# Layer 2, second block: the products with w_ch1 of a step, then its products with w_ch2 in one stretch

## The chip, the cores and the metric

One core of a Trainium2 chip runs the whole program. The metric is the device time of one execution in microseconds (us), the median of several. TensorE (PE) does the matmuls, VectorE (DVE), ScalarE (ACT) and GpSimd (POOL) the work around them, and SyncE (SP) issues every DMA of the kernel from one queue, in program order.

## The reference, cut to what matters

A retention layer makes `x` of 4 batches of 576 rows and 512 columns; a first gated layer (w_in, w_sg, w_out) follows, and then layer 2, which the change is about:

```python
xn = (x - mean) / sqrt(var + 1e-6) * g_ln            # over the 512 columns
out = x + maximum(xn @ w_ch1, 0) @ w_ch2             # w_ch1: 512 x 2048, w_ch2: 2048 x 512
```

All results are wanted near float32 accuracy. The kernel splits every operand of a matmul into a high half (rounded by the copy) and a low half (operand minus high half), and does three matmuls in place of one: high by high, high by low, low by high.

## The kernel before

The 2304 rows of layer 2 are 18 tiles of 128, in three blocks of six (`TB`). Each block goes through eight steps `p`, so there are 24 steps `s`; a step makes 256 of the 2048 hidden columns for the block.

**The products with w_ch1** are done with seven block products in place of eight (Strassen-Winograd). `hidden(s)` does them: each of the seven is six matmuls of 384 columns into a PSUM bank, 42 matmuls in all, and DVE and ACT put the seven together. The order is w = 0, 5 | 1, 2 | 3, 4 | 6, with a `yield` at each bar. `relu` writes the high half of one of the four hidden tiles (ACT) and its low half (DVE, line 1176).

**The products with w_ch2** of blocks 0 and 1 are `project(s, q)`, q = 0 to 3: nine matmuls of 512 columns each, into six banks that a block holds for all its eight steps (`o_t`). So two of the eight banks are left for the products with w_ch1 in steps 1 to 16. In the main loop each of the four parts of `hidden(s)` is followed by one `project(s - 1, q)`, in steps 1 to 16. Block 2 (steps 16 to 23) is done by `hidden_kept`, which keeps its hidden values, and `multiply_kept` does their products with w_ch2 after step 23.

**What runs beside it.** `split_w2` makes the halves of a 128 x 512 piece of w_ch2 (ACT line 944, POOL line 945), `load_w2` fetches the next piece, `save_w2` writes the halves back to DRAM for block 2, `fetch_w1` brings the split w_ch1 two steps ahead. `turning` prepares combinations of w_ch2 for block 2: load, four subtractions (POOL, line 961), four copies (ACT, line 964), four subtractions (POOL, line 967), store. `ahead(blk, q)` with q from 0 to 31 prepares the next block: rows are loaded and normalized (`norm`: DVE, POOL and ACT), turned (DVE, line 994), stored (`z_dram`), loaded as features, scaled, mixed (`mix_features`, POOL line 1029) and split (`split_features`, ACT line 1036, low half on line 1037 by DVE for block 0 and by POOL for blocks 1 and 2). `load_rest` fetches the rows that the output is added to (DVE, line 1276).

Every engine runs its instructions in the order in which this code emits them; the schedule is written out by hand.

Of the kernel before, what the change touches and what calls it, by code (L numbers as in the profile page):

```python
# [101 lines left out]
def kernel(  # L102
# [36 lines left out]
    def f(ap):  # L139
        return ap.bitcast(F32)  # L140
# [804 lines left out]
            pool.tensor_tensor(out=t[:, 1], in0=raw, in1=f(t[:, 0]), op=ALU.subtract)  # L945

    def save_w2(s):
        if NF <= s < 2 * NK:
            p, i = divmod(s - NF, 2)
# [23 lines left out]
    def row_tile():  # L973

        rows.rotate(-1)
        return rows[-1]

    def load_y(n):
        yh[n] = row_tile()
        nc.sync.dma_start(out=yh[n], in_=y_dram[n])  # L980

    def norm(p, n):
        z = yh[n]

        def stats():
            st = numbers(p)
            yield from rstd(p, st, z, 1e-6)
            after(1, lambda: newton(st))

            def rest():  # L990
                normed(z, st)
                yield
                t = row_tile()
                dve.transpose(out=t, in_=z)
                nc.sync.dma_start(out=z_dram[n], in_=t)

            after(2, rest)

        after(0, stats)
# [23 lines left out]
    def mixed(i):  # L1023
        return mix_at[i % len(mix_at)].rearrange("p (k q c) -> p k q c", k=2, c=32)
# [6 lines left out]

    def split_features(blk):
        b11, b21, b12, b22 = halves(blk)
        for i, y in ((0, b11), (4, mixed(0)), (5, mixed(1)), (6, mixed(2)), (2, mixed(3)), (1, b21), (3, b22)):
# [138 lines left out]
    def relu(s, i, v):  # L1173
        t = h_t[s, i] = h_at[i][s % len(h_at[i])]
        act.activation(out=t[:, 0], in_=v, func=ACTF.Relu)  # L1175
        dve.scalar_tensor_tensor(  # L1176
            out=t[:, 1], in0=v, scalar=0.0, in1=f(t[:, 0]), op0=ALU.max, op1=ALU.subtract
        )

    def hidden(s):  # L1180


        u = t2.tile([128, TH], F32, tag="u", name="u")
        t = t2.tile([128, TH], F32, tag="v", bufs=1, name="t")
        bk = {}
        for part in ((0, 5), (1, 2), (3, 4), (6,)) if s else ((5, 0, 2, 4), (1,), (3,), (6,)):
            for w in part:
                x, a, first, last = HIDDEN[w]
                if first:
                    bk[a] = bank()  # L1190
                product(s, bk[a], w, x, first, last)
                v = bk[a][:, 0:TH]
                if w == (0 if s else 5):
                    act.copy(u, v)
                elif w in (0, 5):
                    dve.tensor_tensor(out=u, in0=v, in1=u, op=ALU.add)
                elif w == 2 or w == 4:
                    dve.tensor_tensor(out=t, in0=v, in1=u if w == 2 else t, op=ALU.add)
                    if w == 4:
                        relu(s, 3, t)  # L1200
                else:
                    if w != 1:
# [3 lines left out]
                    relu(s, {1: 0, 3: 2, 6: 1}[w], v)  # L1206
                if last:
                    free(bk[a])
            yield

    def hidden_kept(s):

# [35 lines left out]
    def turned_row(t):  # L1248
        return t.rearrange("p (k f c) -> p f k c", k=KE, c=32)
# [9 lines left out]
    def project(s, q):  # L1259

        blk, p = divmod(s, NQ)
        i, h = divmod(q, 2)
        t = h_t.pop((s, q))
        if p == 0 and q == 0:
            o_t[blk] = [bank() for j in range(TB)]
        first, last = p == 0 and i == 0, p == NQ - 1 and i == 1
        w = w2_at[i]
        for j in reversed(range(TB // 2)):
# [3 lines left out]
            if last:  # L1272
                n = blk * TB + h * TB // 2 + j

                o = row_tile()
                dve.tensor_tensor(
                    out=turned_row(o), in0=ps.rearrange("p (f k c) -> p f k c", k=KE, c=32),
                    in1=o_s.pop(n).rearrange("p (f k c) -> p f k c", k=KE, c=32), op=ALU.add,
                )
                free(ps)  # L1280
                store_row(n, o)

    def load_rest(n):
        o_s[n] = row_tile()
# [109 lines left out]
    def ahead(blk, q):  # L1394

        tick()
        background(int(PACE[B][q % 4]) if blk == 0 and q > 3 else 0)
        n = (blk + 1) * TB
        if q == 1 and blk:
            for j in reversed(range(TB // 2, TB)):  # L1400
                load_rest((blk - 1) * TB + j)
        if blk + 1 < NB:
            for j in range(TB):
                at = 3 + 5 * j // 2
                if q == at - (j > 0 and blk):
                    load_y(n + j)
                if q == at + 1 + (blk if j == 0 else 0):
                    norm(t2, n + j)
            if q in (13, 20):
                load_features(blk + 1, q // 20)  # L1410
            if q in (15 + blk, 22 + blk):
# [12 lines left out]
            if q >= 24 and q != 28:  # L1424
                if q > 24:
                    next(feat[0], None)
                next(feat[1])
        if q == 4 * NQ - 1:
            for j in reversed(range(TB // 2)) if blk + 1 < NB else range(TB):
                load_rest(blk * TB + j)  # L1430
            if blk + 1 == NB:
                o_s[None] = row_tile()

    def keep():
        t = t4[0].tile([128, 28 * TH], F32, tag="fe", name="kept")
# [27 lines left out]
    for s in range(NB * NQ):  # L1463
        if s == NK:
            keep()
        steps = hidden(s) if s < NK else hidden_kept(s)
        for q in range(4):
            next(steps)
            if 0 < s <= NK:
                project(s - 1, q)  # L1470
            if s >= NQ:
                next(turns, None)

            if q == 0 and s > 1:
                split_w2(2 * s - 1)
            if q == 1 and s > 1:
                load_w2(2 * s + 1)
                save_w2(2 * s - 1)
            if q == 2 and s:
                split_w2(2 * s)  # L1480
            if q == 3 and s:
                load_w2(2 * s + 2)
                save_w2(2 * s)
            if s and q == 2:
                save_w1(s + 1, 0)
# [8 lines left out]
            if s == NB * NQ - 1:  # L1494
# [4 lines left out]
                if q == 3:  # L1499
                    split_kept(4)  # L1500
                    split_kept(5)
            ahead(*divmod(4 * s + q, 4 * NQ))
            if q < 2 and s:
                split_w1(s + 1, q)
            if s < 2 and q > 1 - s and q < 4 - s:
                save_w1(s, q - 2 + s)
            if q == 0:
                fetch_w1(s + 1, 3)
            else:
                fetch_w1(s + 2, q - 1)  # L1510
    for _ in multiply_kept(NB - 1):
        pass

# [59 lines left out]
```

## Time and profile before

| | us |
|---|---|
| median of 3 runs | 658.28 (658.03 to 658.71) |
| the profiled execution | 658.18 |
| its span, first to last instruction | 656.2 |
| PE busy in the span | 646.8 (99%) |
| DVE, ACT, POOL busy | 455.0, 316.0, 321.6 |
| steps 0 to 23 of layer 2 | 282.03 to 591.72 of the span |
| of these, block 1 and step 16 | 399.26 to 540.73 |

The span is the time between the first and the last instruction; the time of the execution is 2.0 us longer. TensorE's granted clock is at its upper level all along. A matmul's row shows its start and a duration that overlaps that of the next one, so the pace of a run of matmuls is read from the starts, not from the durations.

### The profile page before, as it was taken

The page shows a single profiled execution, that of the slowest core. Times are in us where ns is not written, and L with a number is a line of the kernel's source. Part 1 is how long each engine was busy: PE and PEld are TensorE (multiplying, and loading weights), DVE is VectorE, ACT ScalarE, POOL GpSimd, SP SyncE. Part 2 cuts the span into 40 slices and gives each one's busy share as a digit, 9 for nine tenths or more (in the row PEclk, how much of TensorE's full clock was granted, in tenths as well). Part 3 has the DMA queues.
Part 4 walks back from the last instruction along what each step waited for, and adds up shares of the span by engine and source line. Part 5 has one row for each costly group of instructions (what it writes and reads, how often), then busy time and mean ns, then how long its engine had stood idle before and what let it go on. Part 6 is the DMA issues. An engine that isn't in the chain of part 4 may idle for free.

```text
span 656.2 us, 12551 instructions
## 1 busy us (share of the span) xinstructions
PE 646.8 (99%) x4422; PEld 591.2 (90%) x4422; DVE 455.0 (69%) x906; ACT 316.0 (48%) x656; POOL 321.6 (49%) x315
## 2 busy tenths in 40 slices
PE   8998999999999999999999999999999999999997
PEld 5998899899889889899888999888988899999996
DVE  4698779789989885868888533555533345458894
ACT  4556795365286466434453533233535313335443
POOL 2467868225326528945655793265559743310000
PEclk9999999999999999999999999999999999999999
DMA  8999447777797695489896867799999699999634
GB/s 306 383 368 371 166 111 213 252 238 233 259 298 232 189 242 145 151 312 384 319 309 238 274 205 261 247 366 387 347 332 360 216 295 350 371 379 405 243 129 161
DMA packets 99264, 181.22 MB, mean 276 GB/s; under 512 B 9857, under 2 KB 46849, under 8 KB 97410
## 3 DMA queue, kind: packets, MB, share of 16 engines
q1 hardware_dynamic: 99202, 180.42, 81.5%
q8 instruction: 35, 0.57, 0.3%
q14 instruction: 27, 0.22, 0.1%
HBM read 122.97 MB, written 56.62 MB: 274 GB/s over the span
## 4 chain that ended last, share of the span: by engine, by line
PE 71%; DVE 3%; ACT 3%; DMA 1%; issue 1%; POOL 1%; SPq 0%; POOLq 0%; ACTq 0%; DVEq 0%
PE b L137 20%; PE b L136 20%; PE b L135 20%; PE b L864 4%; PE b L1341 3%; PE b L1342 2%; DVE c L163 1%; DMA raw<-in_w_ch_dram 1%; ACT t L695 1%; PE b L798 1%; POOL vnl L721 1%; PE b L797 0%; ACT t L692 0%; ACT raw L160 0%; DVE bs L669 0%
## 5 line engine op out<-in xcount | busy, mean ns | idle before, releaser
L137 PE MATMUL b<-fe,w 128*128 128x384 f32 x336 | 113.1, 337 | 0.0
L135 PE MATMUL b<-fe,w 128*128 128x384 f32 x336 | 112.9, 336 | 0.0
L136 PE MATMUL b<-fe,w 128*128 128x384 f32 x336 | 112.7, 335 | 0.0
L137 PE MATMUL b<-w,h 128*128 128x512 f32 (+1 forms) x270 | 98.1, 363 | 0.0
L136 PE MATMUL b<-w,h 128*128 128x512 f32 (+1 forms) x270 | 98.0, 363 | 0.0
L135 PE MATMUL b<-w,h 128*128 128x512 f32 (+1 forms) x270 | 96.8, 358 | 0.0
L945 POOL TENSOR_TENSOR w<-raw_w,w 128x512 fp32r<-128x512 f32 x30 | 39.6, 1320 | 59.0 <-ACT w L944 53.3
L135 PEld LDWEIGHTS b<-fe,w 128*128 128x128 f32 x336 | 63.1, 188 | 3.0
L136 PEld LDWEIGHTS b<-fe,w 128*128 128x128 f32 x336 | 63.1, 188 | 2.8
L137 PEld LDWEIGHTS b<-fe,w 128*128 128x128 f32 x336 | 63.0, 188 | 0.0
L137 PEld LDWEIGHTS b<-w,h 128*128 128x128 f32 x270 | 51.0, 189 | 7.6
L160 ACT ACTIVATE raw<-raw 128x512 f32<-128x512 f32 x44 | 29.9, 679 | 56.2 <-DVE b L158 49.3
L136 PEld LDWEIGHTS b<-w,h 128*128 128x128 f32 x270 | 50.9, 189 | 6.3 <-POOL w L945 0.2
L135 PEld LDWEIGHTS b<-w,h 128*128 128x128 f32 x270 | 51.0, 189 | 6.0 <-issue 0.2
L1175 ACT ACTIVATE h<-b 128x384 fp32r<-128x384 f32 x32 | 15.7, 492 | 83.8 <-DVE b L1204 54.1
L665 POOL TENSOR_TENSOR st<-st,par 128x1 f32<-128x1 f32 x36 | 22.1, 617 | 52.7 <-DVE st L664 52.2
L1176 DVE SCALAR_TENSOR_TENSOR h<-b,h 128x384 fp32r<-128x384 f32 x32 | 17.8, 556 | 30.9 <-ACT h L1175 30.9
L137 PE MATMUL b<-w_sg,vnl 128*128 128x288 f32 x128 | 37.8, 295 | 0.2 <-POOL vnl L721 0.2
L135 PE MATMUL b<-w_sg,vnh 128*128 128x288 f32 x128 | 37.8, 295 | 0.0
L137 PE MATMUL b<-xt_hi,w_in 128*128 128x288 f32 x128 | 37.7, 295 | 0.0
L136 PE MATMUL b<-w_sg,vnh 128*128 128x288 f32 x128 | 37.7, 295 | 0.0
L136 PE MATMUL b<-xt_lo,w_in 128*128 128x288 f32 x128 | 37.7, 294 | 0.0
(199 smaller groups left out, 1700.8 us busy)
## 6 DMA issues: line engine op xcount, KB each, us to landing
w<-ws_dram SPq DMA_DIRECT2D x96, 256.0 KB, 4.8
raw<-in_w_ch_dram SPq DMA_DIRECT2D x32, 512.0 KB, 5.0
ws_dram<-w SPq DMA_DIRECT2D x16, 896.0 KB, 7.4
w<-wb_dram SPq DMA_DIRECT2D x14, 1024.0 KB, 5.6
qv<-in_attn_dram SPq DMA_DIRECT2D x15, 576.0 KB, 6.8
w_dram<-c SPq DMA_DIRECT2D x32, 256.0 KB, 3.1
wb_dram<-fe SPq DMA_DIRECT2D x32, 256.0 KB, 5.1
kk<-in_attn_dram SPq DMA_DIRECT2D x15, 544.0 KB, 7.7
```

The lines of the kernel that those rows point to most:

```text
L135: pe.matmul(ps, lh, rh, start=first, stop=False, skip_group_check=True)
L136: pe.matmul(ps, lh, rl, start=False, stop=False, skip_group_check=True)
L137: pe.matmul(ps, ll, rh, start=False, stop=last, skip_group_check=True)
L160: act.activation(out=f(w1), in_=f(w1), func=ACTF.Square)
L163: dve.scalar_tensor_tensor(out=f(c), in0=f(w1), scalar=F64_LEAST ** 2, in1=f(r), op0=ALU.is_ge, op1=ALU.mult)
L665: pool.tensor_tensor(out=st[:, 4:5], in0=st[:, 3:4], in1=col(par, O_MH), op=ALU.pow)
L864: pe.matmul(ps, g, wo[k][:, w], start=done[0] == 1, stop=done[0] == 3 * KE, skip_group_check=True)
L945: pool.tensor_tensor(out=t[:, 1], in0=raw, in1=f(t[:, 0]), op=ALU.subtract)
L1175: act.activation(out=t[:, 0], in_=v, func=ACTF.Relu)
L1176: dve.scalar_tensor_tensor(out=t[:, 1], in0=v, scalar=0.0, in1=f(t[:, 0]), op0=ALU.max, op1=ALU.subtract)
L1341: pe.matmul(ps, e[:, 0, x], t, start=begin, stop=False, skip_group_check=True)
L1342: pe.matmul(ps[:, 0:256], e[:, 1, x], t[:, 0:256], start=False, stop=end, skip_group_check=True)
```

## The change

In block 1 (steps 8 to 15) `hidden_once(s)` does all seven products with w_ch1, 42 matmuls, in the order 0, 5, 1, 2, 4, 3, 6, and then `project(s, q, 1)` of the same step follows for q = 3, 2, 0, 1, 36 matmuls. Step 7's own w_ch2 products come in one go after step 7. Before, they all came one step later, between the parts.

- The number, size and operands of the matmuls stay. Except in the last step of the block, the nine matmuls of a `project` go high by high for its three rows, then high by low, then low by high.
- The low halves come later than the high ones (`relu_low`); for hidden tile 0 the maximum is first written to SBUF (`z`).
- Both pieces of w_ch2 of a step are split after the second product of the step, and the next two are loaded there.
- The low halves of block 2's features go from POOL to DVE, in another order; the steps of `mix_features` and `split_features` shift by a q here and there.
- `turning` for a piece starts every five q rather than four, with four q between load and first use; half of the `save_w2` pieces are written in block 0.
- `z_dram` stores of block 2's rows are gathered and issued at the end of a step or ahead of the feature loads (`store_z`); `load_rest` is issued at q = 28 and 29 for all six rows.

```diff
     def split_features(blk):
...
-            (pool if blk else dve).tensor_tensor(out=lo, in0=y, in1=f(hi), op=ALU.subtract)
+            (pool if blk == 1 else dve).tensor_tensor(out=lo, in0=y, in1=f(hi), op=ALU.subtract)
...
+    def hidden_once(s):
+        u = t2.tile([128, TH], F32, tag="u", name="u")
+        t = t2.tile([128, TH], F32, tag="v", bufs=1, name="t")
+        z = t2.tile([128, TH], F32, tag="z", bufs=1, name="z")
+        bk = {}
+        for w in (0, 5, 1, 2, 4, 3, 6):
+            x, a, first, last = HIDDEN[w]
+            if first:
+                bk[a] = bank()
+            product(s, bk[a], w, x, first, last)
+            v = bk[a][:, 0:TH]
+            if w == 0:
+                act.copy(u, v)
+            elif w == 1:
+                dve.tensor_scalar(out=z, in0=v, scalar1=0.0, scalar2=None, op0=ALU.max)
+            elif w == 2 or w == 4:
+                dve.tensor_tensor(out=t, in0=v, in1=u if w == 2 else t, op=ALU.add)
+                if w == 2:
+                    relu(s, 0, z)
+                else:
+                    relu(s, 3, t)
+            elif w == 3:
+                dve.tensor_tensor(out=v, in0=v, in1=u, op=ALU.add)
+                relu(s, 2, v)
+                relu_low(s, 3, t)
+            else:
+                dve.tensor_tensor(out=u, in0=v, in1=u, op=ALU.add)
+                if w == 6:
+                    relu(s, 1, u)
+            if last and w != 3:
+                free(bk[a])
+            if w == 5:
+                yield
+        relu_low(s, 2, bk[2][:, 0:TH])
+        free(bk[2])
+        relu_low(s, 0, z)
+        relu_low(s, 1, u)
+        yield
...
+        for x, y in ((0, 0), (0, 1), (1, 0)) if begin and not last else ():
+            for j in js:
+                pe.matmul(
+                    o_t[blk][h * TB // 2 + j], t[:, x, j * 128:(j + 1) * 128], w[:, y], start=first and x == y,
+                    stop=False, skip_group_check=True,
+                )
...
-            start, pace = (3 + 4 * p, 1) if p < 5 else (8 * p - 8, 2)
-            for o in (0, 1, 1, 2, 2, 3, 4, 5):
+            start, pace = (3 + 5 * p, 1) if p < 6 else (8 * p - 15, 2)
+            for o in (0, 4, 4, 5, 5, 8, 8, 9) if p < 6 else (0, 1, 1, 2, 2, 3, 4, 5):
...
-        steps = hidden(s) if s < NK else hidden_kept(s)
+        if s < NQ:
+            steps = hidden(s)
+        elif s < NK:
+            steps = hidden_once(s)
+            next(steps)
+            split_w2(2 * s + 1)
+            split_w2(2 * s)
+            load_w2(2 * s + 3)
+            load_w2(2 * s + 2)
+            next(steps)
+        else:
+            steps = hidden_kept(s)
         for q in range(4):
-            next(steps)
-            if 0 < s <= NK:
+            if NQ <= s < NK:
+                project(s, (3, 2, 0, 1)[q], 1)
+            else:
+                next(steps)
+            if 0 < s < NQ:
                 project(s - 1, q)
...
+        store_z()
+        if s == NQ - 1:
+            split_w2(2 * s + 1)
+            load_w2(2 * s + 3)
+            save_w2(2 * s + 1)
+            for q in range(4):
+                project(s, q)
```

## Rows read from the trace of the kernel before

**Rows 1.** The page's first part: busy time, share of span, instructions of each engine.
```profile
PE 646.8 (99%) x4422; PEld 591.2 (90%) x4422; DVE 455.0 (69%) x906; ACT 316.0 (48%) x656; POOL 321.6 (49%) x315
```

**Rows 2.** Waits of PE, first and last of four: total us, times, longest.
```profile
PE b L519 <- ACT zero L515: 2.3, 1, 2.3
...
PE b L137 <- POOL vnl L721: 0.2, 1, 0.2
```

**Rows 3.** Windows: steps 11, 18, 9, then block 1 with step 16.
```profile
core 0: us, PE busy (x) PEld busy (x) DVE busy (x) ACT busy (x) POOL busy (x), PEclk, DMA share, GB/s
446.49:462.20 15.71, 15.71 (x80) 14.14 (x78) 7.58 (x21) 5.68 (x12) 9.60 (x13) 1.00 1.08 359
548.04:555.32 7.28, 7.28 (x44) 7.28 (x44) 3.83 (x7) 3.10 (x9) 3.34 (x5) 1.00 1.02 349
414.97:430.78 15.81, 15.81 (x79) 14.07 (x78) 8.33 (x18) 5.25 (x12) 5.80 (x7) 1.00 0.96 316
399.26:540.73 141.47, 141.47 (x703) 127.16 (x702) 64.84 (x138) 50.84 (x103) 80.80 (x80) 1.00 0.95 319
```

**Rows 4.** Timeline of PE, layer 1: start us, us; first and end of 48 matmuls.
```profile
221.80 0.62 PE L864 MATMUL b<-w_out,glh 128*128 128x512 f32 x2
...
232.68 0.39 PE L135 MATMUL b<-w_in,xt_hi 128*128 128x512 f32 x1
```

**Rows 5.** Timeline of PE, step 12: the turns between the two shapes.
```profile
464.30 0.39 PE L135 MATMUL b<-w,h 128*128 128x512 f32 x1
...
466.38 0.33 PE L135 MATMUL b<-fe,w 128*128 128x384 f32 x1
...
467.45 0.33 PE L135 MATMUL b<-fe,w 128*128 128x384 f32 x1
...
468.49 0.39 PE L135 MATMUL b<-w,h 128*128 128x512 f32 x1
```

**Rows 6.** Timeline of PE, step 9, third group of w_ch2 products.
```profile
425.69 0.50 PE L136 MATMUL b<-w,h 128*128 128x512 f32 x1
426.03 0.40 PE L137 MATMUL b<-w,h 128*128 128x512 f32 x1
...
426.73 0.39 PE L137 MATMUL b<-w,h 128*128 128x512 f32 x1
...
427.41 0.39 PE L137 MATMUL b<-w,h 128*128 128x512 f32 x1
```

**Rows 7.** Timeline, step 18: ACT's copy of product 0, DVE's add of product 2.
```profile
549.40 0.48 ACT L1225 COPY u<-b 128x384 f32<-128x384 f32 x1
552.39 0.56 DVE L1231 TENSOR_TENSOR t<-b,u 128x384 f32<-128x384 f32 x1 [1.45 <-PE b L137]
```

**Rows 8.** Timeline of DVE around step 8: two low halves, three row adds.
```profile
398.59 1.42 DVE L1176 SCALAR_TENSOR_TENSOR h<-u,h 128x384 fp32r<-128x384 f32 x1 [0.65 <-ACT h L1175]
405.30 0.56 DVE L1176 SCALAR_TENSOR_TENSOR h<-b,h 128x384 fp32r<-128x384 f32 x1 [3.10 <-ACT h L1175]
412.11 2.25 DVE L1276 TENSOR_TENSOR row<-b,row 128x512 f32<-128x512 f32 x3
```

**Rows 9.** Timeline of POOL at the change of blocks.
```profile
397.74 3.97 POOL L1037 TENSOR_TENSOR fe<-x,fe 128x768 fp32r<-128x768 f32 x2
401.67 1.30 POOL L945 TENSOR_TENSOR w<-raw_w,w 128x512 fp32r<-128x512 f32 x1
```

**Rows 10.** Groups of instructions of POOL, 399.26 to 540.73: busy, mean ns.
```profile
L945 POOL TENSOR_TENSOR w<-raw_w,w 128x512 fp32r<-128x512 f32 x17 | 22.0, 1297 | 34.7 <-ACT w L944 28.9 <-DMA z_dram<-row 5.2 <-DMA w<-ws_dram 0.5
L961 POOL TENSOR_TENSOR raw_turn<-raw_turn 128x256 f32<-128x256 f32 x24 | 17.7, 739 | 21.2 <-DMA raw_turn<-w_dram 19.7 <-DMA raw_w<-w_dram 0.6
L1029 POOL TENSOR_TENSOR mix<-x,mix 128x768 f32<-128x768 f32 x2 | 3.7, 1840 | 0.0
```

**Rows 11.** Line 1037 on DVE, layer 1's end: duration min, median, max.
```profile
L1037 DVE TENSOR_TENSOR fe<-x_raw,fe x5: 951/1925/2231, 255.3 to 279.0; 128x768 fp32r<-128x768 f32 x5
```

**Rows 12.** A group of ACT's instructions, 399.26 to 540.73: busy, mean ns.
```profile
L944 ACT CAST w<-raw_w 128x512 fp32r<-128x512 f32 x17 | 10.5, 618 | 0.1
```

More of the change, by code (lines that the diff above doesn't have):

```diff
@@ L947, in save_w2 @@
     def save_w2(s):
-        if NF <= s < 2 * NK:
-            p, i = divmod(s - NF, 2)
+        if NQ <= s < NF + NQ:
+            p, i = divmod(s % NF, 2)
             for h in range(1 + i):
@@ L980, in load_y, with store_z @@
         nc.sync.dma_start(out=yh[n], in_=y_dram[n])
+    z_out = []
+    def store_z():
+        for n, t in z_out:
+            nc.sync.dma_start(out=z_dram[n], in_=t)
+        z_out.clear()
     def norm(p, n):
@@ L994, in rest @@
                 dve.transpose(out=t, in_=z)
-                nc.sync.dma_start(out=z_dram[n], in_=t)
+                z_out.append((n, t))
+                if p is t1 or n < 2 * TB:
+                    store_z()
             after(2, rest)
@@ L1033, in split_features @@
         b11, b21, b12, b22 = halves(blk)
-        for i, y in ((0, b11), (4, mixed(0)), (5, mixed(1)), (6, mixed(2)), (2, mixed(3)), (1, b21), (3, b22)):
+        m = [(4, mixed(0)), (5, mixed(1)), (6, mixed(2)), (2, mixed(3))]
+        for i, y in [(0, b11)] + (m + [(1, b21), (3, b22)] if blk < 2 else [(1, b21), (3, b22)] + m):
             hi, lo = (t.rearrange("p (k q c) -> p k q c", k=2, c=32) for t in fe[blk][i])
             act.copy(hi, y)
-            (pool if blk else dve).tensor_tensor(out=lo, in0=y, in1=f(hi), op=ALU.subtract)
+            (pool if blk == 1 else dve).tensor_tensor(out=lo, in0=y, in1=f(hi), op=ALU.subtract)
             yield
@@ L1175, in relu, with relu_low @@
         act.activation(out=t[:, 0], in_=v, func=ACTF.Relu)
+    def relu_low(s, i, v):
+        t = h_t[s, i]
         dve.scalar_tensor_tensor(
@@ L1206, in hidden @@
                     relu(s, {1: 0, 3: 2, 6: 1}[w], v)
+                    relu_low(s, {1: 0, 3: 2, 6: 1}[w], v)
                 if last:
@@ L1209, in hidden @@
             yield
+    def hidden_once(s):
[22 more added lines that the diff above has]
+                relu(s, 2, v)
+                relu_low(s, 3, t)
+            else:
[11 more added lines that the diff above has]
+        yield
     def hidden_kept(s):
@@ L1257, in store_row, with project @@
             nc.sync.dma_start(out=out[b, NC * C:], in_=o[R:])
-    def project(s, q):
+    def project(s, q, begin=0):
         blk, p = divmod(s, NQ)
@@ L1263, in project @@
         t = h_t.pop((s, q))
-        if p == 0 and q == 0:
+        if blk not in o_t:
             o_t[blk] = [bank() for j in range(TB)]
-        first, last = p == 0 and i == 0, p == NQ - 1 and i == 1
+        first, last = p == 0 and i == begin, p == NQ - 1 and i != begin
         w = w2_at[i]
-        for j in reversed(range(TB // 2)):
+        js = list(reversed(range(TB // 2)))
+        for x, y in ((0, 0), (0, 1), (1, 0)) if begin and not last else ():
[4 more added lines that the diff above has]
+                )
+        for j in () if begin and not last else js:
             c = slice(j * 128, (j + 1) * 128)
@@ L1271, in project @@
             mm3(ps, t[:, 0, c], t[:, 1, c], w[:, 0], w[:, 1], first, last)
[L1272 to L1281, printed above, removed]
+            if not last:
+                continue
+            n = blk * TB + h * TB // 2 + j
+            o = row_tile()
+            dve.tensor_tensor(
+                out=turned_row(o), in0=ps.rearrange("p (f k c) -> p f k c", k=KE, c=32),
+                in1=o_s.pop(n).rearrange("p (f k c) -> p f k c", k=KE, c=32), op=ALU.add,
+            )
+            free(ps)
+            store_row(n, o)
     def load_rest(n):
@@ L1398, in ahead @@
         n = (blk + 1) * TB
-        if q == 1 and blk:
-            for j in reversed(range(TB // 2, TB)):
-                load_rest((blk - 1) * TB + j)
+        if q in (28, 29) and blk + 1 < NB:
+            for j in reversed(range(TB // 2)):
+                load_rest(blk * TB + (q - 28) * TB // 2 + j)
         if blk + 1 < NB:
@@ L1408, in ahead @@
                     norm(t2, n + j)
-            if q in (13, 20):
-                load_features(blk + 1, q // 20)
-            if q in (15 + blk, 22 + blk):
+            if q in (13, 20 - blk):
+                store_z()
+                load_features(blk + 1, q // 19)
+            if q in (15 + 2 * blk, 22 + blk):
                 scale_features(blk + 1, q // 20)
@@ L1423, in ahead @@
                 next(feat[0])
-            if q >= 24 and q != 28:
+            if blk:
+                if q == 25:
+                    next(feat[0])
+                if q >= 24 and q != 29:
+                    next(feat[1])
+                if q in (27, 28):
+                    next(feat[0])
+            elif q >= 24 and q != 28:
                 if q > 24:
@@ L1427, in ahead @@
                 next(feat[1])
-        if q == 4 * NQ - 1:
-            for j in reversed(range(TB // 2)) if blk + 1 < NB else range(TB):
+        if q == 4 * NQ - 1 and blk + 1 == NB:
+            for j in range(TB):
                 load_rest(blk * TB + j)
-            if blk + 1 == NB:
-                o_s[None] = row_tile()
+            o_s[None] = row_tile()
     def keep():
@@ L1465 @@
             keep()
-        steps = hidden(s) if s < NK else hidden_kept(s)
-        for q in range(4):
-            next(steps)
-            if 0 < s <= NK:
+        if s < NQ:
[10 more added lines that the diff above has]
+            steps = hidden_kept(s)
+        for q in range(4):
+            if NQ <= s < NK:
[3 more added lines that the diff above has]
+            if 0 < s < NQ:
                 project(s - 1, q)
-            if s >= NQ:
+            if s >= NK:
                 next(turns, None)
[L1474 to L1482, printed above, removed]
+            if s < NQ:
+                if q == 0 and s > 1:
+                    split_w2(2 * s - 1)
+                if q == 1 and s > 1:
+                    load_w2(2 * s + 1)
+                    save_w2(2 * s - 1)
+                if q == 2 and s:
+                    split_w2(2 * s)
+                if q == 3 and s:
+                    load_w2(2 * s + 2)
+                    save_w2(2 * s)
+            elif q == 1:
+                save_w2(2 * s + 1)
                 save_w2(2 * s)
@@ L1502 @@
             ahead(*divmod(4 * s + q, 4 * NQ))
+            if NQ <= s < NK:
+                next(turns, None)
             if q < 2 and s:
@@ L1510 @@
                 fetch_w1(s + 2, q - 1)
+        store_z()
+        if s == NQ - 1:
+            split_w2(2 * s + 1)
+            load_w2(2 * s + 3)
+            save_w2(2 * s + 1)
+            for q in range(4):
+                project(s, q)
     for _ in multiply_kept(NB - 1):
```

## The prediction

> **What bounds the kernel now.** Start with the page's first part: PE is busy for 99% of the span [rows 1]. Then PE's waits: there are four, and they lie in layer 1 and before it; the first is the longest with 2.3 us, the last has 0.2 us [rows 2]. So no wait of any size is left in layer 2. A busy PE is not a PE at its best pace, though, and the next view is the time from one start to the next. In layer 1, 48 matmuls of 512 columns in a row take 232.68 - 221.80 = 10.88 us, 0.2267 us each [rows 4]. Step 18 has only its 42 matmuls of 384 columns and takes 7.28 us, 0.1733 us each [rows 3]. Step 11 has 42 of these and 36 of 512 columns. At these two paces it would take 7.28 + 36 x 0.2267 = 15.44 us; it takes 15.71 [rows 3]. The 0.27 us between them are not a wait that any view names, and the clock is at its upper level (1.00) in all these windows.
>
> Where they are is seen inside step 12. Nine matmuls of 512 columns after a run of 384 take 466.38 - 464.30 = 2.08 us, at the even pace 2.04. The six of 384 that follow take 1.07, the next six 1.04 [rows 5]. So each turn from one shape to the other slows the matmuls behind it, and a step has four pairs of turns: 0.27 / 4 = 0.067 us a pair. That the w_ch2 matmuls themselves can run at 0.227 is seen in step 9. There a late operand holds one matmul up (0.34 us from start to start) and, some matmuls later, three take 427.41 - 426.73 = 0.68 us [rows 6].
>
> **What the change takes away.** From step 8 to step 16 there are now nine steps with four pairs each, 141.47 us [rows 3]. After it: step 7's w_ch2 products join those of step 6, 36 x 0.2267 = 8.16; steps 8 to 15 have one pair each, 8 x (7.28 + 8.16 + 0.067) = 124.06; step 16 has no w_ch2 products, 7.28, and 0.03 for the one turn. Sum 139.53, gain 1.94 us. Of this, 0.10 is step 9's hold-up (15.81 against 15.71), which goes because the load of a piece to be turned gets four q of time; POOL's subtractions waited 19.7 us for such loads in this stretch [rows 3, 10]. Number and shapes of matmuls stay; I cost the new order of the nine (three rows in turn) at nothing, since every matmul loads its operand before as after (4422 loads for 4422 matmuls [rows 1]). I know no row with that order. If a bank's change cost 0.005 us each, as much as a turn costs a matmul, 8 x 36 of them would cost 1.4; if it gained as much, 1.4 the other way. The 48 matmuls of rows 4 change their bank several times without a trace, so zero is nearest.
>
> The Trainium skill says otherwise: by its page "TensorE: Matmul & The Clock Gate", section "Back-to-back issue gap", the spacing of full-speed matmuls hangs only on their own columns (columns over 2.4 GHz and some 2.5 ns), 162.5 and 215.8 ns here. The paces of rows 3 and 4 are 11 ns above this, and rows 5 show what it has no place for, a dependence on the matmuls before. By it a turn costs nothing and the gain is only the 0.10.
>
> **What the change puts in: less cover.** Times below are from a step's start. A product takes 1.04 us (six times 0.1733), and only two banks are free for seven products, so a bank must be emptied while one other product runs. Step 18 shows just this turn: product 2 ends at 548.04 + 4 x 1.04 = 552.20, DVE starts at 552.39 and needs 0.56, to 552.95, and the next product into that bank starts at 553.24 without a slower pace [rows 3, 7]. ACT's copy of product 0 (0.48) has as much room. The slack is 0.29 us where a projection of 2.08 us lay before. I cost it at nothing as long as DVE and ACT are free when a product ends. Bounds: 0, and 0.2 us in each of eight steps (a rival, below).
>
> The halves for w_ch2: ACT's copy of u starts at about 1.3; the two casts (0.62 each [rows 12]) follow, and POOL makes the two low halves (1.30 each [rows 10]) from 2.3 to 4.9. The first matmul needing one comes at about 8.0. Hidden tile 3 is summed at 5.95, its high half is there by 6.6, wanted at 7.3. Its low half is queued on DVE at 6.9, wanted six matmuls after 7.3, at 8.7. That leaves 1.2 us for 0.56.
>
> Two places don't fit. A low half with both inputs in SBUF waited for POOL's instruction in flight: 1.42 us in place of 0.56, ending 0.45 after POOL's first 2 us on line 1037, while one that reads a bank took 0.56 [rows 8, 9]. **Step 14**: POOL goes from the two low halves straight to two mixes of 1.84 us [rows 10], 4.9 to 6.7 and 6.7 to 8.5. DVE's low half queued at 6.9 meets the second and ends at 8.9, 0.2 us late. Bounds 0 (it slips between the mixes) and 0.5 (the mix has just begun). **Step 16**: in step 15 DVE adds the rows of the last two projections (2.25 us for three [rows 8], pitch 0.78), and block 2's last two feature halves are queued behind the first and the second three. The second three start when the sixth half ends, at the end of step 15, so the last half runs from 2.35 to 3.30 of step 16 at the 0.95 that line 1037 takes undisturbed [rows 11]. Its matmul comes at 3.15 + 0.17 = 3.32. A POOL instruction of 0.74 [rows 10] in flight makes it up to 0.7 late, two of them 1.5. POOL is turning w_ch2 then; I take half of one, 0.3 us late.
>
> **Other edges, at nothing.** Step 7's second w_ch2 piece is split by POOL behind two feature halves until 401.67 + 1.30 = 402.97 [rows 9]; its matmul comes 19 matmuls after 399.26, at 403.57. If POOL were 2 us later, 1.4 us would show. Features' low halves leave POOL and give DVE seven instructions of 0.95 to 2.23 [rows 11], four of them in step 14: 4 to 9 us, against some 8 between DVE's last hidden half (9.9) and its first add of the next step (17.8). On SP, the mid-step loads of w_ch2 wait for POOL's low halves, and fetches of w_ch1, saves, and row loads stand behind them; w_ch1 comes two steps ahead, so they have a step to spare. The z stores wait for DVE's turning; at the step's end only the next step's loads are behind them, before they stood in the middle. Steps 16 and 17 now follow within 14.6 us: 3.7 MB of w_ch1, 1.6 of output, 1.6 of turning, 6.9 MB. At the 349 GB/s of step 18 [rows 3] that is 19.8 us, 5.2 late, less than the 7.28 of a step that the fetch has ahead.
>
> **Sum.** 658.18 for the profiled execution (span 656.2 and 2.0 around it), minus 1.94, plus 0.2 and 0.3: 656.74. The median of the runs is 0.10 above the profiled one, so 656.8 us.
>
> **The rivals.**
> - *Nothing waits.* DVE finds POOL idle in steps 14 and 16: 656.3.
> - *The banks come late in every step.* DVE or ACT still has work of the step before when the first product ends; 0.29 us of slack is soon used. At 0.2 us a step, 1.6: 658.4. For: DVE, ACT and POOL pass work on to each other for each normalized row. Against: step 18, and DVE is busy for 7.58 of the 15.71 us of step 11 [rows 3].
> - *A turn costs nothing, or the cost moves elsewhere*, as by the skill's rule: gain 0.10, waits 0.5: 658.7. Against: rows 5 and 6.
> - *Slower: DVE's background no longer fits.* In steps 9 to 12 DVE must do its share of the six normalizations between 9.9 and 17.8. That is 2.6 us of work (7.58 less nine hidden instructions of some 0.55), but each row waits for POOL and ACT in between, and the turning's four subtractions can stand ahead of POOL's part. PE used to cover such waits with a projection; now the first add of the next step would be late and PE would stand for a bank. Every us beyond 17.8 in these four steps costs four. From 0.7 us a step it is slower than before by the bound; at 0.9 it is 660.4.
>
> **How the numbers follow.** Two medians tell a change apart from about 0.2% (1.3 us), that is below 657.0 or above 659.6. The forecast case has 0.62 (two short waits, 656.3 to 657.7), three quarters of it below 657.0. Nothing waits 0.06; late banks 0.14, four fifths within; turn without price 0.08, within; slower 0.10, nine tenths of it beyond. So faster 0.52, same 0.36, slower 0.12. The range 656.2 to 658.6 takes in the bounds of both waits, late banks up to 0.2 us and half of the free turn. The forecast's own range is 656.3 to 657.7.
>
> **What would show it.** Steps 9 to 13 of 15.51 us each, with one slower stretch after each turn; block 1 with step 16 some 1.4 us shorter; a PE gap of about 0.2 us in step 14 at hidden tile 3's low half and one of about 0.3 in step 16 at product 2. Wrong if w_ch2 matmuls in a run of 36 don't settle at 0.227 us, or if PE's waits list DVE or ACT in steps 8 to 13.

## The result and the profile after

The changed kernel is slower. Its median is 666.12 us (664.21 to 666.9, six runs), that of the kernel before on the same chip 658.5 (657.78 to 659.97, six runs). The ratio is 1.0108, with a 95% interval of 1.0089 to 1.0126 (of all runs, so not quite the quotient of the two medians). The profiled execution took 664.21, with a span of 662.4.

The page after: its first part (busy time, share of the span, instructions), the row of the clock over 40 slices of the span, and three of PE's waits (total, times, longest).

```profile
PE 648.5 (98%) x4422; PEld 592.7 (89%) x4422; DVE 463.6 (70%) x921; ACT 317.3 (48%) x656; POOL 311.6 (47%) x308
PEclk9999999999999999999999999999999997999999
PE b L135 <- ACT u L1281: 5.0, 1, 5.0
PE b L519 <- ACT zero L515: 2.3, 1, 2.3
PE b L136 <- DVE fe L1047: 0.7, 1, 0.7
```

PE's busy time rose by 1.7 us against [rows 1], with as many matmuls. The row of waits is the more telling: [rows 2] had none in layer 2, and now one of 5.0 us leads the list. The clock has one slice at 7 tenths; it is the slice that holds this wait.

Windows after: steps 9, 16, 18 and 19, to be read beside [rows 3].

```profile
core 0: us, PE busy (x) PEld busy (x) DVE busy (x) ACT busy (x) POOL busy (x), PEclk, DMA share, GB/s
421.71:437.22 15.51, 15.51 (x79) 14.07 (x78) 7.65 (x21) 3.59 (x7) 5.07 (x6) 1.00 0.77 250
530.43:538.75 8.32, 7.60 (x43) 7.28 (x42) 6.12 (x9) 1.73 (x4) 5.32 (x6) 1.00 0.98 336
546.04:561.52 15.48, 10.38 (x43) 9.74 (x43) 3.83 (x7) 3.50 (x9) 8.57 (x13) 0.78 0.99 336
561.52:568.80 7.28, 7.28 (x43) 7.28 (x43) 3.83 (x7) 1.99 (x5) 1.51 (x3) 1.00 1.03 361
```

Step 9 has the forecast 15.51. Steps 10 to 15 took 15.53 or 15.54, and step 8 took 15.51. So block 1 went as predicted. Step 16 is 1.0 longer than a bare step, and step 18, a step that the change does not touch, took 15.48 in place of 7.28.

The account of layer 2, from the starts of the steps: 309.69 us before, 317.49 after, 7.8 more. The new order of the products gave the expected -1.94, 0.10 of it step 9's hold-up. Against it stand 8.2 in step 18, 1.0 in step 16, 0.2 in steps 8 to 15 and 0.4 in block 0 (steps 4 and 5; block 0 is taken up below). Layer 1 ended 1.6 us earlier in this execution than in the one of [rows 2], so that the span grew by 6.2 only.

**What stands still in step 18.** The timeline of PE there (start, us, line, tiles; in brackets the wait and what ended it):

```profile
548.40 0.34 PE L137 MATMUL b<-fe,w 128*128 128x384 f32 x1
553.71 0.69 PE L135 MATMUL b<-fe,w 128*128 128x384 f32 x1 [4.97 <-ACT u L1281]
554.20 0.52 PE L136 MATMUL b<-fe,w 128*128 128x384 f32 x1
554.52 0.52 PE L137 MATMUL b<-fe,w 128*128 128x384 f32 x1
...
559.00 0.40 PE L136 MATMUL b<-fe,w 128*128 128x384 f32 x1
559.24 0.34 PE L137 MATMUL b<-fe,w 128*128 128x384 f32 x1
```

Product 1 is added into the bank that holds product 0, and so it waits until ACT has copied product 0 out (`u`). After the wait the starts are 0.32 us apart (554.20 to 554.52), where they were 0.1733; from 559.00 on the step is at the upper level again (0.24 there, then 0.17). Sixteen matmuls at 0.32 are 2.35 us more than at 0.1733. The window's granted clock of 0.78 is this: after 5 us without a matmul PE went on at the lower of its two levels, 1.2 GHz, and then came back to 2.4. Of the 0.85 that the 8.2 us leave beside these two, about 0.5 were lost at the start of the step, where a fetch of w_ch1 came late, and the rest where PE started again.

**Why ACT is late.** ACT, then POOL, then SP's queue in the same stretch:

```profile
540.42 1.33 ACT L964 CAST fe<-raw_turn 128x256 fp32r<-128x256 f32 x4
...
550.99 0.40 ACT L964 CAST fe<-raw_turn 128x256 fp32r<-128x256 f32 x1 [4.71 <-DMA wb_dram<-fe]
551.71 0.41 ACT L964 CAST fe<-raw_turn 128x256 fp32r<-128x256 f32 x1 [0.31 <-DMA wb_dram<-fe]
552.30 0.41 ACT L964 CAST fe<-raw_turn 128x256 fp32r<-128x256 f32 x1 [0.19 <-POOL fe L967]
552.88 0.41 ACT L964 CAST fe<-raw_turn 128x256 fp32r<-128x256 f32 x1 [0.17 <-DMA wb_dram<-fe]
553.19 0.47 ACT L1281 COPY u<-b 128x384 f32<-128x384 f32 x1
```

```profile
544.62 1.55 POOL L961 TENSOR_TENSOR raw_turn<-raw_turn 128x256 f32<-128x256 f32 x2 [8.64 <-DMA raw_turn<-w_dram]
546.13 2.82 POOL L967 TENSOR_TENSOR fe<-raw_turn,fe 128x256 fp32r<-128x256 f32 x4
```

```profile
540.59 5.02 SPq L931 DMA_DIRECT2D w<-ws_dram  x8
546.89 3.20 SPq L970 DMA_DIRECT2D wb_dram<-fe  x4
```

The copy of product 0 stands behind the four casts of `turning`'s piece 6. These casts write four staging buffers, the same ones for every piece, and each has to wait until the store of piece 5 has left its buffer. Piece 5 was cast at 540.42; its stores were issued from 546.89 on, and the first buffer came free at 550.99, 10.6 us after the cast. The new schedule puts the two casts at q = 36 and 39. That is three q, and a q in block 2 is a fourth of 7.28 us: 5.5 us for a round of some 10. In the kernel before the same two were eight q apart (q = 38 and 46, by `8 * p - 8` and the offsets), 14.6 us.

### The profile page after: what moved, and what is told of

It is laid out like the page before. It is cut to its first block, busy times and chain, and to the rows that moved or that the text cites. A ratio compares the mean times of both kernels' runs of the same rounds, so it can differ in the third digit from the quotient of the medians.

```text
span 662.4 us, 12582 instructions
## 1 busy us (share of the span) xinstructions
PE 648.5 (98%) x4422; PEld 592.7 (89%) x4422; DVE 463.6 (70%) x921; ACT 317.3 (48%) x656; POOL 311.6 (47%) x308
## 4 chain that ended last, share of the span: by engine, by line
PE 70%; DVE 4%; ACT 3%; DMA 1%; issue 1%; POOL 1%; DVEq 0%; ACTq 0%; POOLq 0%
PE b L137 17%; PE b L135 17%; PE b L136 17%; PE b L1327 9%; PE b L864 4%; PE b L1405 3%; PE b L1406 2%; DVE c L163 1%; DVE b L158 1%; DVE b L154 1%; DMA w<-ws_dram 1%; DMA wb_dram<-fe 1%; POOL vnl L721 1%; PE b L798 1%; ACT t L695 0%
## 5 line engine op out<-in xcount | busy, mean ns | idle before, releaser
L135 PEld LDWEIGHTS b<-fe,w 128*128 128x128 f32 x336 | 63.9, 190 | 7.9 <-ACT u L1281 5.3
L136 PEld LDWEIGHTS b<-fe,w 128*128 128x128 f32 x336 | 63.9, 190 | 2.4 <-DVE fe L1047 1.0
L137 PEld LDWEIGHTS b<-fe,w 128*128 128x128 f32 x336 | 63.8, 190 | 0.4 <-DMA w<-ws_dram 0.4
L1327 PE MATMUL b<-w,h 128*128 128x512 f32 x270 | 62.8, 390 | 0.0
L137 PE MATMUL b<-w,h 128*128 128x512 f32 (+1 forms) x180 | 62.3, 346 | 0.0
L136 PE MATMUL b<-w,h 128*128 128x512 f32 (+1 forms) x180 | 62.2, 346 | 0.0
L135 PE MATMUL b<-w,h 128*128 128x512 f32 (+1 forms) x180 | 61.8, 343 | 0.0
L1327 PEld LDWEIGHTS b<-w,h 128*128 128x128 f32 x270 | 50.6, 188 | 10.2
L137 PE MATMUL b<-xt_hi,w_in 128*128 128x288 f32 x128 | 37.7, 295 | 0.0
L137 PEld LDWEIGHTS b<-w,h 128*128 128x128 f32 x180 | 34.1, 189 | 4.1
L135 PE MATMUL b<-xt_hi,w_in 128*128 128x288 f32 x128 | 37.7, 294 | 0.0
L135 PEld LDWEIGHTS b<-w,h 128*128 128x128 f32 x180 | 34.1, 190 | 3.5 <-issue 0.2
```

The lines of the kernel that those rows point to most:

```text
L135: pe.matmul(ps, lh, rh, start=first, stop=False, skip_group_check=True)
L136: pe.matmul(ps, lh, rl, start=False, stop=False, skip_group_check=True)
L137: pe.matmul(ps, ll, rh, start=False, stop=last, skip_group_check=True)
L1327: pe.matmul(o_t[blk][h * TB // 2 + j], t[:, x, j * 128:(j + 1) * 128], w[:, y], start=first and x == y, stop=False, skip_group_check=True,)
```

## The experiments

Theory A of the first experiments was that POOL's order delays the buffers: piece 5's low halves (546.13) stand behind piece 6's first subtractions, which wait 8.64 us for their load. Theory B was that moving the turning later only puts the queues elsewhere. All ratios are to the kernel before on the same chip, with their 95% interval. Where there is none, it is a single run.

**Piece 6 and 7 five q later** (x1).
```diff
-            start, pace = (3 + 5 * p, 1) if p < 6 else (8 * p - 15, 2)
+            start, pace = (3 + 5 * p, 1) if p < 6 else (8 * p - 10, 2)
```


> The last two pieces of w_ch2 to be turned start five q later (8p - 10 in place of 8p - 15); nothing else. Theory A (order): in step 17 the sixth piece's low halves stand on POOL behind the seventh's first subtractions, which wait for their load; so the sixth's stores go out late, ACT's casts of the seventh wait for the staging buffers, ACT's copy of product 0 of step 18 stands behind the casts, and PE waits 5.1 us and then runs 3.1 us slower at the lower clock. With the seventh piece after the sixth all 8.2 us go: step 18 back to 7.28 us, 8 us less than the changed kernel, 656 to 658 us. Theory B (crowding): without the projections steps 16 to 18 have too many transfers for their time, and something is late whatever the order: PE still waits some us in steps 17 to 20, over 661 us.

657.47 us, ratio 0.9994 (0.9981 to 1.0007). Windows of steps 18 and 19:

```profile
546.77:554.05 7.28, 7.28 (x44) 7.28 (x44) 3.83 (x7) 1.99 (x5) 0.00 (x0) 1.00 1.02 364
554.05:562.81 8.76, 8.01 (x44) 7.15 (x44) 3.83 (x7) 3.41 (x9) 5.74 (x8) 1.00 1.04 361
```

Step 18 is back to 7.28, and the loss is gone with it. Step 19 lost 1.5 instead, and PE's wait there is for a fetch of w_ch1 (0.7): a small part of what theory B foresaw.

**Only the load of piece 6 earlier** (x2).
```diff
-            for o in ... if p < 6 else (0, 1, 1, 2, 2, 3, 4, 5):
+            for o in ... if p < 6 else (-2 if p == 6 else 0, 1, 1, 2, 2, 3, 4, 5):
```


> The seventh piece's load alone goes four q earlier (q = 29 in place of 33); its subtractions, casts and stores stay. Theory A: POOL's first subtractions of that piece no longer wait 8.6 us, the sixth piece's low halves follow at once, its stores go out some 5 us earlier, and the 5.1 us wait of step 18 shrinks to 0 to 1 us; 656 to 658 us. Theory B: the stores land as late as before, because the queue is full: the wait stays at 4 to 5 us, over 662 us.

663.63 us in a single run, and step 18 took 14.8. ACT's casts of piece 6 and SP's queue:

```profile
551.10 0.41 ACT L964 CAST fe<-raw_turn 128x256 fp32r<-128x256 f32 x1 [4.69 <-DMA wb_dram<-fe]
```

```profile
538.79 5.94 SPq L931 DMA_DIRECT2D w<-ws_dram  x10
544.83 3.88 SPq L970 DMA_DIRECT2D wb_dram<-fe  x4
```

Theory A's link fell. With the load early POOL no longer stands in the way, yet the buffer comes free at the same time, 551.10 against 550.99. The low halves were 4.6 us earlier (541.57 against 546.13), the stores only 2.1 (SP stood in ten fetches of w_ch1 until 544.73), and the first of them then took 6.3 us until its buffer was free, in place of 4.1. That is what theory B expected. What both kernels share is the distance between the two casts, and this took theory A's place.

**The old schedule of `turning` in the changed kernel** (x3).
```diff
-            start, pace = (3 + 5 * p, 1) if p < 6 else (8 * p - 15, 2)
-            for o in (0, 4, 4, 5, 5, 8, 8, 9) if p < 6 else (0, 1, 1, 2, 2, 3, 4, 5):
+            start, pace = (3 + 4 * p, 1) if p < 5 else (8 * p - 8, 2)
+            for o in (0, 1, 1, 2, 2, 3, 4, 5):
```


> Turning goes by the schedule of the kernel before (every four q, first use one q after the load, the last three pieces from q = 32); all else as in the changed kernel. Theory A: the pieces of block 2 are in order again, so step 18 does not wait; but POOL waits for loads in block 1 again, now with the low halves of w_ch2 for the same step behind it, so small waits of 0.1 to 2 us come up in steps 9 to 13; 656 to 662 us. Theory B: step 17 to 20 still wait, over 662 us.

665.33 us in a single run. Windows of steps 13, 14 and 18, and ACT in step 14:

```profile
484.35:502.15 17.80, 15.79 (x80) 14.02 (x79) 5.81 (x11) 5.82 (x12) 7.64 (x10) 1.00 0.85 258
502.15:525.10 22.95, 17.92 (x80) 16.16 (x78) 8.75 (x14) 10.03 (x19) 11.40 (x10) 0.85 0.85 294
555.37:562.64 7.27, 7.27 (x43) 7.27 (x43) 3.83 (x7) 3.09 (x9) 2.83 (x4) 1.00 0.99 333
```

```profile
505.00 0.78 ACT L964 CAST fe<-raw_turn 128x256 fp32r<-128x256 f32 x2 [9.68 <-DMA wb_dram<-fe]
...
508.94 0.46 ACT L1240 COPY u<-b 128x384 f32<-128x384 f32 x1
```

Step 18 is right, but the same wait now stands in block 1: casts behind a store (9.68 us), a copy of product 0 behind the casts, PE waiting in step 13 (2.0) and step 14 (5.0), where 0.1 to 2 us were expected. So the reordered block needs another schedule for `turning` than before, and the one it was given fails only at its end.

**As x1, and block 2's features in six q without a gap** (x4).
```diff
-                if q >= 24 and q != 29:
+                if 24 <= q < 31:
```


> As the first, and block 2's last two feature halves go one q earlier each (q = 29 and 30 in place of 30 and 31), so the last is ahead of the second three row adds on VectorE. In the changed kernel PE waited 0.9 us at product 2 of step 16 and lost 0.1 more in the turn. Theory A, with the prediction's reason for that wait: step 16 takes 7.31 us in place of 8.33, another 1.0 us less than the first kernel here, 655 to 657 us, faster than the kernel before. Rival: the half was late because POOL holds the port, not because of the row adds; then at most 0.3 us of it goes.

656.63 us, ratio 0.999 (0.9973 to 1.0007). Windows of steps 16 and 19:

```profile
531.25:538.56 7.31, 7.31 (x44) 7.30 (x42) 4.63 (x8) 1.74 (x4) 5.41 (x7) 1.00 0.98 317
553.12:561.48 8.36, 8.03 (x44) 7.14 (x43) 3.83 (x7) 3.39 (x9) 5.74 (x8) 1.00 1.02 353
```

Step 16 costs its bare 7.31 when the last feature halves are emitted a q earlier. So the 1.0 us there came from them. In x1, x2, x3 and x7, with the features as in the changed kernel, step 16 lost 0.2 to 0.4; the 1.0 is the largest of five profiles. The median of x4 is the lowest of all kernels, but the interval of its ratio holds 1.

**Three pieces late, each eight q apart** (x5): x4 with `(3 + 5 * p, 1) if p < 5 else (8 * p - 8, 2)`.

> The last three pieces of w_ch2 to be turned go by the old schedule (from q = 32, 40 and 48, two q a part); block 2's last two feature halves go early as in the fourth run. Theory A (staging): what PE met in step 18 is ACT's casts waiting for the staging buffers; the sixth piece's own casts, late behind the fifth's store, were part of it. Six and eight q between casts leave room, and the loads no longer crowd steps 17 and 18, so steps 16 to 23 take 7.28 to 7.31 us each, the 1.1 us of step 19 in the fourth run goes, layer 2 takes 308.5 us and the ratio to the kernel before is 0.997 (1.9 us less). Theory B (crowding): some 1 us comes up elsewhere in steps 17 to 22, ratio 0.999.

657.02 us, ratio 0.9991 (0.9974 to 1.0008). No better: steps 17, 18, 20, 22 and 23 lost 0.2, 0.5, 0.6, 1.1 and 0.4 us. In steps 18 and 23 PE's weight loads wait for w_ch1; in steps 20 and 22 they wait for w_ch1 and also for ACT's copy of product 0, which still stands behind casts (PE idle for 0.5 and 0.6). So theory B held, and theory A's eight q did not take the casts' delay away altogether.

**As x5, with all stores of w_ch2's halves in block 1** (x6).
```diff
-        if NQ <= s < NF + NQ:
-            p, i = divmod(s % NF, 2)
+        if NF <= s < 2 * NK:
+            p, i = divmod(s - NF, 2)
```


> As the fifth run, but all halves of w_ch2 are written to DRAM in block 1, none in block 0. Theory: the 0.3 us that step 5 lost in all five profiles with the changed schedule (16.0 in place of 15.71 us) come from the saves that the change moved into block 0, so step 5 is back at 15.71, and block 1 takes the 3 MB without a wait: 0.3 us less than the fifth run. Rival: step 5's loss comes from something else and stays; or block 1's split of w_ch2 waits for the saves, 0.1 to 1 us in steps 12 to 15.

661.1 us, ratio 1.0057 (1.0036 to 1.0079). ACT in step 14:

```profile
501.70 2.13 ACT L1024 ACTIVATE x<-x,par 128x384 f32<-128x384 f32 x4 [8.27 <-DMA x<-z_dram]
503.74 0.46 ACT L1240 COPY u<-b 128x384 f32<-128x384 f32 x1
```

The same pattern with another transfer: the scaling of block 2's features waits 8.27 us for their load, the copy of product 0 waits behind it, and PE behind that (2.9). Step 14 took 20.07, and neither the theory nor the rival had named this wait. The stores that the change moved to block 0 are therefore worth having there. Steps 4 and 5 took 15.71 and 15.69 here, but in x5 too, so their loss in the first profile is not shown to come from the moved stores.

**The casts of pieces 6 and 7 on POOL** (x7).
```diff
-            act.copy(t[:, 0], x)
+            pool.tensor_copy(t[:, 0], x) if p > 5 else act.copy(t[:, 0], x)
```


> The changed kernel, but the four casts of the seventh and the eighth piece to be turned are done by GpSimd in place of ScalarE; schedule and transfers stay. Theory A: PE stood in step 18 only because ScalarE's copy of product 0 was queued behind the casts. With the casts on GpSimd nothing of the step's products is queued behind them: step 18 takes under 8 us in place of 15.49, 656 to 659 us. Theory B: PE waits for something that comes late with the transfers (w_ch1), and step 18 still takes over 11 us.

658.47 us in a single run. Step 18, its copy of product 0 (ACT) and the first cast of piece 6 (now on POOL):

```profile
545.90:554.47 8.57, 7.64 (x44) 7.09 (x43) 4.62 (x9) 2.24 (x5) 6.00 (x11) 1.00 1.04 364
```

```profile
547.33 0.48 ACT L1281 COPY u<-b 128x384 f32<-128x384 f32 x1 [1.18 <-PE b L137]
550.64 0.40 POOL L964 CAST fe<-raw_turn 128x256 fp32r<-128x256 f32 x1 [0.52 <-DMA wb_dram<-fe]
```

The schedule is that of the changed kernel, and the first cast of piece 6 waits for its buffer as before (550.64 against 550.99), but the casts no longer stand in front of ACT's copy, which now waits for PE alone. Of the 8.2 us, 6.9 are gone. The 1.3 left are w_ch1 coming late (PE's longest wait for it is 0.9), where a step under 8 us was expected, 0.7 lost at most; steps 19 to 23 lost another 1.3.

**The kernel before with nothing but the new schedule of `turning`** (x8): the reverse of x3's diff.

> The kernel before with one part of the change alone: the new schedule of turning. Theory A: the three q between the sixth and the seventh piece's casts are too few in steps of 7.3 us whatever block 1 does, so step 18 waits here too; the sixth piece's casts are on time, since step 16 still takes 15.7 us, so it waits less: 1 to 4 us, 659 to 664 us. Rival: the wait needs the whole of the change (the fifth piece's stores held up behind output rows and fetches at the start of step 16); then step 18 takes 7.28 us and the time is that of the kernel before within 0.2%.

665.5 us in a single run, about the time of the whole change, though not by the same sum. Step 18, and ACT in it:

```profile
549.32:562.82 13.50, 8.96 (x43) 8.65 (x43) 3.83 (x7) 3.50 (x9) 4.53 (x7) 0.87 1.02 354
```

```profile
553.34 0.40 ACT L964 CAST fe<-raw_turn 128x256 fp32r<-128x256 f32 x1 [3.78 <-DMA wb_dram<-fe]
...
555.57 0.47 ACT L1225 COPY u<-b 128x384 f32<-128x384 f32 x1
```

So the schedule alone makes this wait without any reordering of products. Step 18 lost 6.2 us, with a wait of PE of 4.5, more than the 1 to 4 expected and less than the 8.2 of the changed kernel. This kernel also lost 2.4 us in step 15, mostly behind POOL's low half of w_ch2 (PE waits 1.6), which was not expected and which the changed kernel doesn't lose.

**As x4, with `turning` starting at q = 0** (x9): `(5 * p, 1)` in place of `(3 + 5 * p, 1)`.

> Changed kernel with the feature halves early and all turning early: pieces 0 to 5 start at q = 5p (in place of 3 + 5p), the last two at 8p - 10. Theory: less of the turning falls into steps 16 to 20, and the piece-to-piece distance of the casts stays at five q or more, so no cast waits for the staging buffers; steps 17 to 22 wait 0 to 0.5 us in all, in place of 1.1 in the fourth run; layer 2 takes 308 to 309 us, ratio 0.997. Rival: any turning in steps of 7.3 us makes w_ch1 late somewhere, 1 to 2 us in all, ratio 0.999.

660.22 us, ratio 1.0035 (1.0022 to 1.0047). A miss: steps 17 and 18 took 9.75 and 8.50, waiting for w_ch1, and step 14 took 16.09.

**Without turning, and before without it** (x10, x11). In both, the body of `turning` stores zeros, four stores a step in block 1, in place of the combinations of w_ch2; x10 also has x4's edit of the features.
```diff
-            at.setdefault(start + o * pace, []).append(p)
...
+        for t in stage:
+            pool.memset(f(t), 0.0)
+        for q in range(4 * NQ):
+            if q % 4 == 2:
+                for j, t in enumerate(stage):
+                    nc.sync.dma_start(out=wb_dram[j, q // 16, :, q // 4 % 4], in_=f(t))
```


> Changed kernel with the feature halves early and without turning: no loads, subtractions, casts; zeros are stored in place of the combinations of w_ch2, all in block 1, so block 2's output lacks what comes from these. Theory: with the turning away, the change is the fewer turns between the shapes alone, and shows its 1.8 to 1.9 us whole: steps 8 to 15 at 15.51 to 15.54 us, step 16 at 7.31, steps 17 to 23 at 7.28 with no wait; layer 2 takes 307.8 us, ratio to the kernel before 0.997, and to the eleventh run the same. Rival: the steps of 7.3 us still wait for w_ch1 as in the fifth run, since w_ch1 alone is 1.8 MB in 7.3 us: 1 us or more of waits in steps 17 to 23.

> The kernel before with the same zeros stored in place of the turned w_ch2, at the same q; the same part of the output is left out. Theory: turning costs the kernel before nothing on PE, so the time is that of the kernel before within 0.1% (layer 2 309.6 us, steps 1 to 16 at 15.71), and the tenth run is 1.8 to 1.9 us faster than this. Rival: turning hides waits of the kernel before too, and this one is 0.5 us or more faster than it.

657.2 us for x10, ratio 0.9998 (0.9988 to 1.0008), and 658.62 for x11, ratio 1.0014 (0.9998 to 1.003). The window of x10 from step 16 to 23, and step 16 of x11:

```profile
532.02:590.28 58.26, 58.26 (x337) 58.26 (x336) 31.88 (x58) 16.48 (x34) 0.00 (x0) 1.00 0.91 311
```

```profile
524.33:540.04 15.71, 15.71 (x80) 14.13 (x78) 6.86 (x12) 2.53 (x6) 3.71 (x3) 1.00 0.92 322
```

58.26 is 8 x 7.28: with `turning` gone block 2 has no wait at all. From step 7 to 23 x10 took 206.85 us and x11 208.05. So the reordering of the products gives 1.2 us of the 1.94 by itself, after step 14 has taken back 0.5 (16.03: the low half that waits for POOL's mix). The medians stand 1.4 apart, but the ratio of 0.997 that was expected of x10 did not come: against the kernel before, on the same chip, it is the same.

**As x4, with the fetch of w_ch1 ahead of `turning`** (x12).
```diff
-            if s >= NK:
-                next(turns, None)
...
+            if s >= NK:
+                next(turns, None)
```


> As the fourth run, and in steps 16 to 23 a q's part of the turning is issued behind that q's w_ch1 fetch, not ahead of it. Theory: step 19's 1.1 us in the fourth run are w_ch1 coming late, because on SP its fetch stood behind the fifth and sixth piece's stores, which wait for GpSimd. With the fetch ahead step 19 takes 7.28 to 7.6 us, layer 2 308 to 308.7 us, and the kernel is faster than the one before: ratio 0.997, interval below 1. Rival: the transfers themselves are too many, whatever their order, and the 1 us stays in step 19 or comes up in step 20 to 23: ratio 0.999.

657.14 us, ratio 0.9997 (0.9981 to 1.0013). Step 19 fell from 8.36 to 7.74 (7.28 to 7.6 was expected), and steps 17, 18 and 20 to 23 took 7.28. Step 14 has the late half (16.01), and step 2 lost 0.86 us.

None of the mended kernels is measurably faster than the one before. Steps 7 to 23 took 208.16 us before, 207.37 in x4 and 207.33 in x12, so 0.8 us are gained there; block 0 lost about as much in the same profiles (0.77 in x4). Block 0 loses up to 1 us from profile to profile, also in x11, where it is that of the kernel before. What causes this stays open.

## Why the prediction was wrong

656.8 us was forecast, within 656.2 to 658.6; it is 666.12.

- **What bounds the kernel, and what the change takes away: right.** Step 7 with its second 36 took 23.87, as forecast (15.71 + 8.16), and steps 8 to 15 took 15.51 to 15.54, forecast 15.51. The run of 36 matmuls of 512 columns takes 8.20 us (36 x 0.2267 + 0.04), in step 8, in the new order, as in step 15, where half are in the old one; so the new order of the nine costs nothing, as taken. The formula that the prediction took from the Trainium skill (page "TensorE: Matmul & The Clock Gate", section "Back-to-back issue gap"), columns over 2.4 GHz and some 2.5 ns, has no place for a turn and would have left 15.71 there; the trace does not agree with it on this point. The section gives the formula for an isolated matmul, though, and says that in a stream of weight loads and matmuls both set the spacing; the prediction read more out of it than that.
- **The banks and the halves for w_ch2: right.** PE has no wait for DVE or ACT in steps 8 to 13. The slack of 0.29 us was enough, and the slower rival, DVE's background in steps 9 to 12, didn't come.
- **Step 14: forecast 0.2, measured 0.** The low half slipped between POOL's mixes, the lower bound. That was luck: ACT's casts of w_ch2 waited 0.8 for their load, so POOL's two low halves began at 3.3 of the step and not at 2.3, and the mixes came later too. In x10 and x12, where they began at 2.35 as worked out, the low half met the second mix as foreseen, and in x9 it met a first mix just begun; these steps took 0.5 to 0.6 more, the upper bound.
- **Step 16: forecast 0.3, measured 1.0**, within the bounds. The three row adds and the halves stand in the order that was foreseen:

```profile
529.77 1.20 DVE L1047 TENSOR_TENSOR fe<-mix,fe 128x768 fp32r<-128x768 f32 x1
530.89 2.25 DVE L1340 TENSOR_TENSOR row<-b,row 128x512 f32<-128x512 f32 x3
533.05 1.53 DVE L1047 TENSOR_TENSOR fe<-mix,fe 128x768 fp32r<-128x768 f32 x1
534.50 0.55 DVE L1283 TENSOR_TENSOR u<-b,u 128x384 f32<-128x384 f32 x1
```

  The last half takes 1.53 us, not 0.95, while POOL is at work (four subtractions of `turning` from 532.22 to 535.99): of the choice "I take half of one" (0.74), 0.58 was due. It also began 0.27 later than worked out. The four other profiles with the same features lost 0.2 to 0.4 here, so 0.3 was near the usual size and this profile's 1.0 is the largest.
- **"Other edges, at nothing": the step that failed.** It followed `turning` through POOL's subtractions and DMAs: its transfers in steps 16 and 17 were summed, its waits for loads were seen, and the change's longer distance between load and use was entered as a gain of 0.10. What it did not follow is the other half of each piece: cast on ACT, low half on POOL, store on SP, and then the same four buffers again. A cast that waits for a store holds whatever ACT has queued behind it, and in block 2 that is the copy of product 0, with a whole step of PE hanging on it. The two lines of the diff give the distance, three q, and step 18's 7.28 us in [rows 3] give its length, 5.5 us; the time from cast to free buffer in the trace of before would have decided it. It can be read there from piece 6, cast 14.6 us after piece 5:

```profile
562.74 1.31 ACT L964 CAST fe<-raw_turn 128x256 fp32r<-128x256 f32 x4
567.06 2.38 SPq L970 DMA_DIRECT2D wb_dram<-fe  x4
```

  The first of these stores landed at 572.05, 5.0 us after its issue and 9.3 after the cast. A distance of 14.6 us covers that, one of 5.5 does not. x1, x7 and x8 show the cause from three sides: widen the distance, take the casts off ACT, or give the old kernel this schedule alone.
- **The rivals.** None named this mechanism. All took their waits from the work that the new order of products changes, and the loss lies in a step whose products are untouched.

## What to carry to other kernels

When background work gets a new schedule, follow each of its pieces until the buffer is free again, on every engine and queue, and compare the time between two uses with the time of a round; a schedule counted in program steps changes its length where the steps get shorter. An engine that works in order carries each wait of its background to whatever is queued behind it, so keep instructions that may wait for a DMA off the engine that empties the accumulators, or give them enough distance. A gain of 2 us that is right in nearly every step can still be lost elsewhere, so a step that the diff doesn't name needs to be followed as closely as those that it does.

## What the runs showed of the hardware

- A turn between matmuls of 384 and 512 columns costs 0.067 us a pair, as read from the trace before: steps with four pairs took 15.71, with one pair 15.51.
- After a wait of 5.0 us PE went on at 1.2 GHz for 16 matmuls (0.32 us in place of 0.1733), and after one of 2.9 us in x6 the granted clock fell too; after one of 2.0 us (x3, step 13) it stayed at 1.00. So the wait of 5.0 us cost some 7.7 with what came after it (8.2 less the 0.5 at the step's start).
- With the DMA share at 0.95 in step 17 and 0.99 in step 18, a staging buffer took 10.6 us from cast to free, and 4.1 of it from the first store's issue (546.89) to the cast that it let go (550.99). With the next piece loaded earlier (x2) it was 10.0 (541.09 to 551.10), and the time from issue to free grew to 6.3.
